# A transformer block planned offline: new cost constants for the planner that orders every engine

## Chip, core and metric

The kernel runs on one core of one Trainium2 chip. The metric is the device time of one execution in microseconds. Three runs of the kernel before took 1159.46, 1160.88 and 1164.24, median 1160.88.

## What is computed

One pre-norm transformer block over 2048 tokens of width 1024, batch 1, in bf16. Attention has 32 query heads of width 32 that share one key head and one value head. The feed-forward part has width 3584 and a sigmoid gate.

```python
def _A_ref(x, wq, wk, wv, wo):                      # H = 32, Dh = 32
    q = (x @ wq).reshape(B, S, H, Dh) ...           # x is layer-normed
    k = x @ wk ; v = x @ wv                         # one head for all
    p = softmax(einsum("bhqd,bkd->bhqk", q, k) * Dh ** -0.5)
    return einsum("bhqk,bkd->bhqd", p, v) ... @ wo

def _B_ref(x, w_gate, w_up, w_down):
    return (sigmoid(x @ w_gate) * (x @ w_up)) @ w_down

h  = x + _A_ref(_layernorm(x), wq, wk, wv, wo)
h2 = h + _B_ref(_layernorm(h), w_gate, w_up, w_down)
```

## The kernel before

Tokens are cut into 16 tiles of 128. Attention goes through *visits*. A visit is one step over 256 keys for two groups of four heads and one token tile: eight score matmuls into PSUM (`S_ps`, written by `emit_S`) and two exponentials of 128x1024 on ScalarE (line 571, `exps`) that write the tile `Pr`. There are 512 visits, 32 per token tile, and 1024 exponentials. `S_ps` has three pairs of banks, and a visit uses two of them, so the scores of a visit wait for the first exponential of the visit before (`deps.append(exps[2 * v - 2])` in `s_ready`).

Everything else that TensorE does is fitted between the scores of successive visits:

- PV blocks (`mk_PV`, `emit_PV`): 32 matmuls of `Pr` with the values `Vb`, two blocks for each eight visits. The second of the two also has eight matmuls with `ones` that sum the running totals `Ts`, from which the softmax's denominators come. `Ts` is added up on VectorE (line 601). When a block is done, VectorE empties its bank: line 633 for the first block; lines 637 and 639 (`Oc`, `Rc`) for the second.
- "Z" matmuls (named `zone` in the first part of the program): key, value and query projections of the whole sequence.
- OP (`mk_OP`): 16 matmuls per token tile with `wo_sb`.
- GU (`mk_GU`): gate and up projection, 14 groups of eight 512-wide matmuls per token tile. Their weights come in pieces of 256 KB over SP's queue (line 775) into the slots `ring` and, at the end, `Pr`. The gate half is followed by a tanh on ScalarE (line 817), the up half by a multiplication on VectorE (line 821), and a transposing DMA (line 825) turns the product for the next step.
- D (`mk_D`): down projection, two groups of 28 matmuls per token tile, with `hact` and `zone`.

PV, Z, OP, GU and D share two PSUM banks (`F_ps`): a group runs into one bank while the other is emptied. TensorE executes in order, so what waits there holds up all that stands behind it, the next scores included.

The order of all engines is written when the program is built, by the class `Plan`. Each operation has a cost: `occ`, how long it holds its engine, and `lat`, when its result is there. The planner advances a clock per engine and picks what its costs say is ready. The main loop emits the scores of a visit when ScalarE's planned backlog is under 750 ns, and otherwise takes a matmul of the group at hand. Where nothing is ready in the plan it emits filler matmuls (`ident` with `kT`) or lets its clock go on. Loads of weight pieces are put in line by `pump`, which looks at the planned state of the DMA queue; each load then waits for the matmul that frees its slot and for one exponential (`beat`). At run time only the order and the semaphores remain; the planned times are gone.

The functions that give the costs are `t_act` (ScalarE), `t_dve` (VectorE) and `t_mm` (TensorE); scores and PV blocks have costs of their own in `emit_S` and `emit_PV`, among them a sum added to `pl.free["pe"]` for the switch between kinds of matmul; a DMA's cost stands in `Plan.step`, from the bytes that its issuer names.

Of the kernel before, what the change touches and what calls it, by code (L numbers as in the profile page):

```python
# [13 lines left out]
P = 128  # L14
DH = 32
LN_EPS_BF16 = 1.0013580322265625e-05
SEM = 75.0
# [19 lines left out]
class Plan:  # L37
# [39 lines left out]
    def step(self, limit):  # L77
        best = None
        for e in self.ENG:
            h = self.heap[e]  # L80
            if h:
                s = max(self.free[e], min(o.ready for o in h))
                if best is None or s < best[0]:
                    best = (s, e)
        if best is None or (limit is not None and best[0] > limit):
            return False
        s, e = best
        h = self.heap[e]
        o = min((o for o in h if o.ready <= s + 1e-9), key=lambda o: (o.prio, o.seq))
        h.remove(o)  # L90
        self.free[e] = s + o.occ
        if o.nbytes:
            go = max(s + 1300.0, self.dma_free[e])
            self.dma_free[e] = go + o.nbytes / 280.0
            o.end = self.dma_free[e] + 700.0
        else:
            o.end = s + o.lat
        o.pos = len(self.lists[e])
        self.lists[e].append(o)
        for u in o.users:  # L100
# [14 lines left out]


def t_act(n):
    return dict(occ=n / 1.2 + 93.0, lat=n / 1.2 + 186.0 + SEM)


def t_dve(n, rate=0.96, fix=158.0):
# [1 line left out]


def t_mm(n):
    return dict(occ=max(25.0, n / 2.4 + 2.0), lat=max(25.0, n / 2.4 + 2.0) + 170.0 + SEM)


def bass_sequential_preLN__grouped_kv_mqa__glu_gated_glu__prompt_kernel(
# [12 lines left out]
    Bsz, S, D = A_x.shape  # L142
# [6 lines left out]
    FW = 512  # L149
# [11 lines left out]
    NST = 3  # L161
# [7 lines left out]
    with ExitStack() as es:  # L169
# [18 lines left out]
        hn = SB("hn", [D])  # L188
        hnT = SB("hnT", [2, DT, P])
# [212 lines left out]

        def dma_xT(t):
            xT_ev[t] = dma(lambda: SP.dma_start_transpose(
                out=xnT4[t // 4][:, :, (t % 4) * P:(t % 4 + 1) * P], in_=x_sb[:, t, :]), f"xT{t}", P * D * 2,
                [xnorm[t]], prio=0, occ=1330.0)
            xT_pe[t] = xT_ev[t]
            queue_after_xT(t)
# [138 lines left out]
        def emit_S(v):  # L547
            G, kq = visits[v]
            qb, g = G // ND, 2 * (G % ND)
            deps = s_ready(v)  # L550
            pl.free["pe"] += 95.0
            last = None
            for kk in range(KB):
                for j in range(4):
                    kt = kq * KB + kk
                    bank = 2 * ((2 * v + j // 2) % NB) + j % 2
                    last = pl.op("pe", mm(S_ps[:, bank, kk * 256:(kk + 1) * 256], kT4[DH * j:DH * (j + 1), kt * P:(kt + 1) * P],
                                          QTb[DH * j:DH * (j + 1), qb % 2, g:g + 2, :], True, True,
                                          tile_position=(DH * j, 0)),
                                 deps if (kk == 0 and j == 0) else [], occ=27.3, lat=27.3 + 190.0 + SEM)  # L560
            pl.free["pe"] += 95.0
            for i in range(2):
                u = 2 * v + i
                slot = u % NPS
                own = slot_owner.get(slot)
                free = [pv_done[own], slot_add[slot]] if own is not None else []
                slot_owner[slot] = (G, kq // VPH)
                slot_add[slot] = None
                slot_of[(G, kq, i)] = slot
                pb = 2 * (u % NB)  # L570
                exps[u] = pl.op("act", lambda slot=slot, pb=pb: ACT.activation(  # L571
                    out=Pr[:, slot, :].rearrange("p (a b) -> p a b", a=2), in_=S_ps[:, pb:pb + 2, :],
                    func=ACTF.Exp, scale=SCALE), [last] + free, prio=3, **t_act(1024))
# [92 lines left out]
        def emit_PV(t):  # L666

            banks = [b for b in range(2) if (cur is None or b != cur_b) and known(bank_rel[b], t)]
            if not banks or not queues["PV"]:
                return False  # L670
            gr = queues["PV"][0]
            if not gr.gate() or not known(gr.first(), t):
                return False
            queues["PV"].popleft()
            b = min(banks, key=lambda b: max([0.0] + [o.end for o in bank_rel[b]]))
            deps = gr.first() + list(bank_rel[b])
            for fn in gr.atoms(b):
                o = pl.op("pe", fn, deps, occ=27.3, lat=27.3 + 220.0 + SEM)
                o.tag = "PV"
                deps = []  # L680
            pl.free["pe"] += 95.0
            bank_rel[b] = gr.after(b, o)
            return True

# [40 lines left out]
        def flush_hT():  # L725
            while late_hT and (late_hT[0] < 2 or (late_hT[0] - 2) in gu_last):
                t = late_hT.pop(0)
                hT_ev[t] = dma(lambda t=t: SP.dma_start_transpose(
                    out=hnT[:, t % 2, :, :], in_=hn[:, :]), f"hT{t % 2}", P * D * 2,
                    [hnorm[t], gu_last.get(t - 2)], prio=0, occ=1330.0)  # L730
                for i in range(NI):
                    queues["GU"].append(mk_GU(t, i))
# [55 lines left out]
        def mk_GU(t, i):  # L788
            p, w = ITEMS[t * NI + i]
            n = t * NFP + i // 2  # L790
            its = [(p, w, d) for d in range(NPI)]

            def ready():
                if not all(it in held and piece_ld[it] for it in its):
                    return None
                return [piece_ld[it][0] for it in its]

            def atoms(b):
                sl = [held[it] for it in its]
# [12 lines left out]
            def after(b, last):  # L812
                if i == NI - 1:
                    gu_last[t] = last
                    flush_hT()
                if w == 0:
                    tanh_of[n] = pl.op("act", lambda: ACT.activation(  # L817
                        out=tnh[:, n % 2, :], in_=F_ps[:, b, :], func=ACTF.Tanh, scale=0.5),
                        [last, tn_user.get(n % 2)], prio=1, **t_act(FW))
                    return [tanh_of[n]]  # L820
                e = pl.op("dve", lambda: DVE.scalar_tensor_tensor(  # L821
                    out=hst[:, n % NST, :], in0=tnh[:, n % 2, :], scalar=1.0, in1=F_ps[:, b, :],
                    op0=ALU.add, op1=ALU.mult), [last, tanh_of[n], st_ev.get(n - NST)], prio=0, **t_dve(FW))
                tn_user[n % 2] = e
                st_ev[n] = dma(lambda: SP.dma_start_transpose(
                    out=hactT[:, t % 2, 4 * p:4 * p + 4, :], in_=hst[:, n % NST, :]), f"ha{n % NST}", P * FW * 2,
                    [e] + ([d_last[t - 2]] if t > 1 else q_store[-NQS:]), prio=0, occ=800.0)
                for f in range(4 * p, 4 * p + 4):
                    hact_ev[(t, f)] = st_ev[n]
                if i == NI - 1:  # L830
                    for dc in range(2):
                        queues["D"].append(mk_D(t, dc))
                return [e]
            gr = Group("GU", atoms, lambda: [hT_ev[t]] + ready()[:2], after)
            gr.gate = lambda: ready() is not None and (q_left[0] == 0 if t == 0 else (t < 2 or d_done[t - 2] == 2))
            return gr
# [217 lines left out]
```

## Time and profile before

| what | value |
|---|---|
| median of three runs | 1160.88 us |
| the profiled execution | 1161.15 us |
| its span, first to last instruction | 1159.4 us |
| granted TensorE clock, mean | 0.995 |
| TensorE / ScalarE / VectorE busy | 93% / 90% / 76% |
| DMA queue of SP, share of 16 engines | 73.4% |
| moved by DMA | 226.79 MB |

The page splits the span by engine, follows back the chain of work that ended last, and groups instructions by line; the groups give the mean length of one instruction, from its start to its end, although neighbours on one engine overlap. The timeline puts instructions of one kind that follow each other into one row: start, length from the first start to the last end, engine, line, names, count, and in brackets the idle time ahead of the row with what ended it. A few per cent of the matmul records are missing, so that a row can have one matmul less than the program. A row of stretches has start and end, length, then for each engine the busy time and the count of instructions, then the granted clock, the DMA share and GB/s; asked for the tile `S_ps`, it counts the score matmuls (TensorE and its weight loads) and the exponentials (ScalarE) alone.

### The profile page before, as it was taken

How to read it: one execution, taken by the hardware profiler on the slowest of the kernel's cores; microseconds unless marked ns; L12 is line 12 of the kernel's file. 1: busy time of each engine (PE TensorE's matmuls, PEld its weight loads, DVE VectorE, ACT ScalarE, POOL GpSimd, SP SyncE). 2: the span in 40 equal slices, each digit the busy share in tenths (PEclk: the TensorE clock that was granted, in tenths of full speed). 3: DMA queues.
4: the chain of work that ended last, by engine and by line, in shares of the span. 5: the costliest groups of instructions: out<-in, count | busy, mean ns of one | idle time of the engine just before them, and what ended most of it. 6: DMA issues, size and time to landing. Idle time of an engine off the chain costs nothing.

```text
span 1159.4 us, 30239 instructions
## 1 busy us (share of the span) xinstructions
PE 1078.7 (93%) x12193; PEld 482.9 (42%) x12374; DVE 877.8 (76%) x1688; ACT 1045.5 (90%) x1167; POOL 55.7 (5%) x84
## 2 busy tenths in 40 slices
PE   9899898889899999999899999999999999999998
PEld 5643344334343443434343443434344433444443
DVE  8889977777787878878697878878797868877511
ACT  6899998989999999999999999999999999999310
POOL 4100000000000000000000000000000000000000
PEclk9999999999999999999999999999999999999999
DMA  8675387876849587785959597785959587776993
GB/s 246 131 240 177 97 260 215 225 217 160 231 118 259 151 222 198 178 234 145 228 123 260 148 226 194 178 234 145 230 121 263 143 227 193 178 223 166 253 269 118
DMA packets 304283, 226.79 MB, mean 196 GB/s; under 512 B 117520, under 2 KB 295440, under 8 KB 304144
## 3 DMA queue, kind: packets, MB, share of 16 engines
q1 hardware_dynamic: 302064, 224.73, 73.4%
q8 instruction: 97, 1.59, 0.6%
q10 hardware_dynamic: 2080, 0.13, 0.1%
q14 instruction: 42, 0.34, 0.1%
HBM read 195.43 MB, written 7.86 MB: 175 GB/s over the span
## 4 chain that ended last, share of the span: by engine, by line
PE 61%; ACT 19%; DMA 7%; DVE 7%; issue 5%; POOL 0%; SPq 0%; POOLq 0%; DVEq 0%; ACTq 0%
PE F_ps L379 50%; ACT Pr L571 18%; PE S_ps L379 11%; DMA ring<-in_B_w_up_dram 6%; DVE Ts L601 3%; ACT tnh L817 1%; DMA ring<-in_B_w_gate_dram 1%; DVE Oc L637 1%; DVE Rc L639 1%; DVE hst L821 0%; DVE Rc L642 0%; DVE hact L267 0%; PE F_ps L384 0%; DVE Ri L640 0%; POOL dsb L339 0%
## 5 line engine op out<-in xcount | busy, mean ns | idle before, releaser
L571 ACT ACTIVATE Pr<-S_ps 128x1024 bf16<-128x1024 f32 x1024 | 979.0, 1029 | 30.9 <-PE S_ps L379 24.2
L601 DVE TENSOR_TENSOR Ts<-Ts,Pr 128x1024 bf16<-128x1024 bf16 x768 | 506.1, 679 | 64.2 <-ACT Pr L571 62.3
L379 PE MATMUL F_ps<-ring,hnT 128*128 128x512 bf16 x1654 | 411.0, 380 | 36.5 <-issue 13.5
L379 PEld LDWEIGHTS F_ps<-ring,hnT 128*128 128x128 bf16 x1760 | 152.0, 98 | 245.1 <-issue 71.9
L379 PE MATMUL S_ps<-QTb,kT 32*128 32x256 bf16 x4096 | 203.8, 273 | 18.7 <-issue 10.4
L379 PE MATMUL F_ps<-zone,hact 128*128 128x512 bf16 x842 | 207.3, 380 | 5.1 <-issue 4.5
L601 DVE TENSOR_TENSOR Ts<-Pr 128x1024 bf16<-128x1024 bf16 x128 | 87.2, 682 | 111.1 <-ACT Pr L571 111.0
L379 PEld LDWEIGHTS S_ps<-QTb,kT 32*128 32x128 bf16 x4096 | 60.7, 92 | 197.6 <-ACT Pr L571 130.4
L379 PE MATMUL F_ps<-Pr,Vb 128*32 128x256 bf16 x4096 | 137.0, 276 | 1.3 <-DVE hact L267 0.9
L379 PEld LDWEIGHTS F_ps<-zone,hact 128*128 128x128 bf16 x896 | 77.9, 98 | 105.8 <-issue 30.9
L817 ACT ACTIVATE tnh<-F_ps 128x512 f32<-128x512 f32 x112 | 68.1, 608 | 50.5 <-PE F_ps L379 50.5
L379 PEld LDWEIGHTS F_ps<-Pr,Vb 128*32 128x32 bf16 x4096 | 98.2, 97 | 33.1 <-issue 17.2
L821 DVE SCALAR_TENSOR_TENSOR hst<-tnh,F_ps 128x512 bf16<-128x512 f32 x112 | 75.4, 673 | 23.3 <-PE F_ps L379 23.1
L379 PE MATMUL F_ps<-zone 128*128 128x256 bf16 (+2 forms) x499 | 74.5, 291 | 5.1 <-DVE hact L267 2.1
L379 PE MATMUL F_ps<-wo_sb,OT 128*128 128x512 bf16 x252 | 62.7, 381 | 8.8 <-DVE Rc L639 7.6
L334 POOL TENSOR_SCALAR zb<-mvb 128x1 bf16<-128x1 bf16 (+1 forms) x25 | 11.7, 469 | 1040.5 <-DVE mvb L330 1040.4
L379 PEld LDWEIGHTS F_ps<-zone 128*128 128x128 bf16 x512 | 37.5, 98 | 33.7 <-issue 8.9
L851 DVE SCALAR_TENSOR_TENSOR h_sb<-F_ps,h_sb 128x512 bf16<-128x512 f32 x32 | 21.6, 677 | 33.9 <-PE F_ps L379 33.9
L379 PEld LDWEIGHTS F_ps<-wo_sb,OT 128*128 128x128 bf16 x256 | 21.4, 98 | 38.2 <-DVE Rc L639 10.7
L637 DVE TENSOR_TENSOR Oc<-F_ps,Oc 128x256 f32<-128x256 f32 x64 | 26.8, 419 | 12.5 <-PE F_ps L379 12.4
L633 DVE COPY Oc<-F_ps 128x256 f32<-128x256 f32 x64 | 27.0, 421 | 10.1 <-PE F_ps L379 9.8
L639 DVE STREAM_TRANSPOSE Rc<-F_ps 128x256 f32<-128x256 f32 x64 | 28.1, 439 | 0.0
(48 smaller groups left out, 359.3 us busy)
## 6 DMA issues: line engine op xcount, KB each, us to landing
ring<-in_B_w_gate_dram SPq DMA_DIRECT2D x320, 256.0 KB, 3.9
ring<-in_B_w_up_dram SPq DMA_DIRECT2D x319, 256.0 KB, 3.6
zone<-in_B_w_down_dram SPq DMA_DIRECT2D x28, 256.0 KB, 3.8
h_sb<-in_A_x_dram SPq DMA_DIRECT2D x16, 256.0 KB, 5.0
out_dram<-h_sb SPq DMA_DIRECT2D x32, 128.0 KB, 3.0
QTb<-q_scratch SPq DMA_DIRECT2D x14, 256.0 KB, 3.9
q_scratch<-hact SPq DMA_DIRECT2D x24, 128.0 KB, 2.5
ring<-in_A_x_dram SPq DMA_DIRECT2D x5, 512.0 KB, 7.0
```

Source lines behind the costliest of these rows:

```text
L334: f = pl.op("pool", lambda: POOL.tensor_scalar(out=zb[:, ph, sl].unsqueeze(2), in0=mvb[:, ph, sl, 1:2], scalar1=LN_EPS_BF16, scalar2=None, ...
L379: return lambda: PE.matmul(o, lhsT=l, rhs=r, start=start, stop=stop, **kw)
L571: exps[u] = pl.op("act", lambda slot=slot, pb=pb: ACT.activation(out=Pr[:, slot, :].rearrange("p (a b) -> p a b", a=2), in_=S_ps[:, pb:pb ...
L601: o = pl.op("dve", lambda T=T, a=a, b=b: DVE.tensor_tensor(out=T, in0=a, in1=b, op=ALU.add), deps, prio=4, **t_dve(1024, 1.92))
L633: oc_ev[G] = pl.op("dve", lambda: DVE.tensor_copy(out=Oc[:, :], in_=O), [last, o_ev.get(G - 1)], prio=0, **t_dve(256))
L637: a = pl.op("dve", lambda: DVE.tensor_tensor(out=Oc[:, :], in0=O, in1=Oc[:, :], op=ALU.add), [last, oc_ev[G]], prio=0, **t_dve(256))
L639: c = pl.op("dve", lambda: DVE.transpose(out=Rc[:, :], in_=R), [last, o_ev.get(G - 1)], prio=0, **t_dve(256))
L817: tanh_of[n] = pl.op("act", lambda: ACT.activation(out=tnh[:, n % 2, :], in_=F_ps[:, b, :], func=ACTF.Tanh, scale=0.5), [last, tn_user.get ...
L821: e = pl.op("dve", lambda: DVE.scalar_tensor_tensor(out=hst[:, n % NST, :], in0=tnh[:, n % 2, :], scalar=1.0, in1=F_ps[:, b, :], op0=ALU.a ...
L851: e = pl.op("dve", lambda: DVE.scalar_tensor_tensor(out=h_sb[:, t % 4, sl], in0=F_ps[:, b, :], scalar=0.5, in1=h_sb[:, t % 4, sl], op0=ALU ...
```

## The change

Only constants of the planner are altered. Nothing is added to or removed from the arithmetic.

| constant | before | after |
|---|---|---|
| exponential of 1024, `occ` | 946 ns | 913 ns |
| tanh of 512, `occ` | 520 ns | 487 ns |
| 512-wide matmul, `occ` | 215.3 ns | 216.0 ns |
| one score matmul, `occ` and the rest of `lat` | 27.3, 265 ns | 27.4, 225 ns |
| one PV matmul, `occ` | 27.3 ns | 27.4 ns |
| behind a visit's scores | 95 ns | 111 ns |
| behind a PV block | 95 ns | 109 ns |
| DMA: start, landing | 1300, 700 ns | 1400, 900 ns |
| bytes named for a transposing DMA | 2 per element | 2.5 per element |
| queue in which a DMA is counted | its issuer's | SP's for all |

```diff
         if o.nbytes:
-            go = max(s + 1300.0, self.dma_free[e])
-            self.dma_free[e] = go + o.nbytes / 280.0
-            o.end = self.dma_free[e] + 700.0
+            go = max(s + 1400.0, self.dma_free["sp"])
+            self.dma_free["sp"] = go + o.nbytes / 280.0
+            o.end = self.dma_free["sp"] + 900.0
...
 def t_act(n):
-    return dict(occ=n / 1.2 + 93.0, lat=n / 1.2 + 186.0 + SEM)
+    return dict(occ=n / 1.2 + 60.0, lat=n / 1.2 + 170.0 + SEM)
...
 def t_mm(n):
-    return dict(occ=max(25.0, n / 2.4 + 2.0), lat=max(25.0, n / 2.4 + 2.0) + 170.0 + SEM)
+    return dict(occ=max(25.0, n / 2.4 + 2.7), lat=max(25.0, n / 2.4 + 2.7) + 170.0 + SEM)
...
-                out=hnT[:, t % 2, :, :], in_=hn[:, :]), f"hT{t % 2}", P * D * 2,
+                out=hnT[:, t % 2, :, :], in_=hn[:, :]), f"hT{t % 2}", P * D * 5 // 2,
...
-                                 deps if (kk == 0 and j == 0) else [], occ=27.3, lat=27.3 + 190.0 + SEM)
-            pl.free["pe"] += 95.0
+                                 deps if (kk == 0 and j == 0) else [], occ=27.4, lat=27.4 + 150.0 + SEM)
+            pl.free["pe"] += 111.0
...
-                o = pl.op("pe", fn, deps, occ=27.3, lat=27.3 + 220.0 + SEM)
+                o = pl.op("pe", fn, deps, occ=27.4, lat=27.4 + 220.0 + SEM)
                 o.tag = "PV"
                 deps = []
-            pl.free["pe"] += 95.0
+            pl.free["pe"] += 109.0
```

The two other transposing DMAs (`dma_xT`, and the one of `hst`) get the same 5 // 2.

What it does to the order is shown on TensorE, at three places of one of the tiles from the middle of the program, which repeat from tile to tile. `S_ps<-QTb,kT` are the scores that begin a visit, `ring,hnT` is GU, `zone,hact` is D, `wo_sb,OT` is OP, `Pr,Vb` and `Ts,ones` are a PV block.

The first place, TensorE at the end of a tile's GU work ahead of D, before the change:

```order
L379 MATMUL S_ps<-QTb,kT 128x256 x8
L379 MATMUL F_ps<-ring,hnT 128x512 x10
L379 MATMUL S_ps<-QTb,kT 128x256 x8
L379 MATMUL F_ps<-ring,hnT 128x512 x5
L379 MATMUL S_ps<-QTb,kT 128x256 x8
L379 MATMUL F_ps<-Pr,Vb 32x256 x32
L379 MATMUL F_ps<-Ts,ones 32x256 x8
L379 MATMUL F_ps<-ring,hnT 128x512
L379 MATMUL S_ps<-QTb,kT 128x256 x8
L379 MATMUL F_ps<-ring,hnT 128x512 x3
```

The same place on TensorE after it:

```order
L379 MATMUL S_ps<-QTb,kT 128x256 x8
L379 MATMUL F_ps<-ring,hnT 128x512 x9
L379 MATMUL S_ps<-QTb,kT 128x256 x8
L379 MATMUL F_ps<-ring,hnT 128x512 x3
L379 MATMUL F_ps<-zone,hact 128x512 x3
L379 MATMUL S_ps<-QTb,kT 128x256 x8
L379 MATMUL F_ps<-zone,hact 128x512 x7
L379 MATMUL S_ps<-QTb,kT 128x256 x8
L379 MATMUL F_ps<-Pr,Vb 32x256 x32
L379 MATMUL F_ps<-Ts,ones 32x256 x8
L379 MATMUL F_ps<-zone,hact 128x512
```

The visits of five and of three GU matmuls are gone; GU work of the tile at hand ends two visits earlier, and the PV block stands beside D.

The second place, TensorE where OP begins, before the change:

```order
L379 MATMUL F_ps<-Pr,Vb 32x256 x32
L379 MATMUL F_ps<-Ts,ones 32x256 x8
L379 MATMUL F_ps<-zone,hact 128x512
L379 MATMUL S_ps<-QTb,kT 128x256 x8
L379 MATMUL F_ps<-wo_sb,OT 128x512 x3
L379 MATMUL S_ps<-QTb,kT 128x256 x8
L379 MATMUL F_ps<-wo_sb,OT 128x512 x7
```

The same place on TensorE after it:

```order
L379 MATMUL F_ps<-Pr,Vb 32x256 x32
L379 MATMUL F_ps<-zone,hact 128x512 x2
L379 MATMUL S_ps<-QTb,kT 128x256 x8
L379 MATMUL F_ps<-zone,hact 128x512 x7
L379 MATMUL S_ps<-QTb,kT 128x256 x8
L379 MATMUL F_ps<-zone,hact 128x512 x2
L379 MATMUL F_ps<-wo_sb,OT 128x512 x4
```

OP stood right behind a block with `ones`, one matmul and one set of scores away; it now follows a block without them, with eleven matmuls and two sets of scores between.

The third place, TensorE in the GU work of the next tile, around the block with `ones`, before the change:

```order
L379 MATMUL S_ps<-QTb,kT 128x256 x8
L379 MATMUL F_ps<-Pr,Vb 32x256 x32
L379 MATMUL F_ps<-Ts,ones 32x256 x8
L379 MATMUL F_ps<-ring,hnT 128x512 x2
L379 MATMUL S_ps<-QTb,kT 128x256 x8
L379 MATMUL F_ps<-ring,hnT 128x512 x6
```

The same place on TensorE after it:

```order
L379 MATMUL S_ps<-QTb,kT 128x256 x8
L379 MATMUL F_ps<-ring,hnT 128x512 x3
L379 MATMUL F_ps<-Pr,Vb 32x256 x32
L379 MATMUL F_ps<-Ts,ones 32x256 x8
L379 MATMUL S_ps<-QTb,kT 128x256 x8
L379 MATMUL F_ps<-ring,hnT 128x512 x5
```

The block now stands behind three GU matmuls of its visit; of the five that follow the scores, two end a group and three begin the next one, in the bank that the block has used.

In the whole program, fillers go from 87 to 57 and weight loads from 655 to 649. Behind the scores of the last visit stand 158 GU matmuls where 148 stood; the numbers of D, OP and PV matmuls there are the same.

More of the change, by code (lines that the diff above doesn't have):

```diff
@@ L404, in dma_xT @@
             xT_ev[t] = dma(lambda: SP.dma_start_transpose(
-                out=xnT4[t // 4][:, :, (t % 4) * P:(t % 4 + 1) * P], in_=x_sb[:, t, :]), f"xT{t}", P * D * 2,
+                out=xnT4[t // 4][:, :, (t % 4) * P:(t % 4 + 1) * P], in_=x_sb[:, t, :]), f"xT{t}", P * D * 5 // 2,
                 [xnorm[t]], prio=0, occ=1330.0)
@@ L825, in after @@
                 st_ev[n] = dma(lambda: SP.dma_start_transpose(
-                    out=hactT[:, t % 2, 4 * p:4 * p + 4, :], in_=hst[:, n % NST, :]), f"ha{n % NST}", P * FW * 2,
+                    out=hactT[:, t % 2, 4 * p:4 * p + 4, :], in_=hst[:, n % NST, :]), f"ha{n % NST}", P * FW * 5 // 2,
                     [e] + ([d_last[t - 2]] if t > 1 else q_store[-NQS:]), prio=0, occ=800.0)
```

## Prediction, made before the changed kernel was run

> **What bounds the kernel now.** I read the page first, then ScalarE and TensorE in order of time inside one token tile, then the stretches between fixed points of the program.
>
> ```profile
> span 1159.4 us, 30239 instructions
> PE 1078.7 (93%) x12193; PEld 482.9 (42%) x12374; DVE 877.8 (76%) x1688; ACT 1045.5 (90%) x1167; POOL 55.7 (5%) x84
> PE 61%; ACT 19%; DMA 7%; DVE 7%; issue 5%; POOL 0%; SPq 0%; POOLq 0%; DVEq 0%; ACTq 0%
> L571 ACT ACTIVATE Pr<-S_ps 128x1024 bf16<-128x1024 f32 x1024 | 979.0, 1029 | 30.9 <-PE S_ps L379 24.2
> ```
>
> TensorE is busy 93%, ScalarE 90%, and the chain that ends last changes between them, so two engines are near their limit. The 1029 ns of one exponential is not its price: in order of time, successive ones overlap.
>
> ```profile
> 424.20 3.77 ACT L571 ACTIVATE Pr<-S_ps 128x1024 bf16<-128x1024 f32 x4
> ...
> 480.51 0.59 ACT L817 ACTIVATE tnh<-F_ps 128x512 f32<-128x512 f32 x1
> 480.99 5.93 ACT L571 ACTIVATE Pr<-S_ps 128x1024 bf16<-128x1024 f32 x6
> ```
>
> Four in 3.77 us make a distance of (3.77 - 1.03) / 3 = 0.913 us; six in 5.93 us make (5.93 - 1.03) / 5 = 0.98, and the additional 0.07 is waiting. So "busy" hides ScalarE's waits, and its real need is 0.913 per exponential and 480.99 - 480.51 = 0.48 per tanh. Where the time goes is seen on TensorE.
>
> ```profile
> 51.32 1.70 PE L379 MATMUL F_ps<-zone 128*128 128x256 bf16 x14
> ...
> 756.80 0.40 PE L379 MATMUL S_ps<-QTb,kT 32*128 32x256 bf16 x8
> 757.13 0.60 PE L379 MATMUL F_ps<-ring,hnT 128*128 128x512 bf16 x2
> 758.04 1.09 PE L379 MATMUL F_ps<-ring,hnT 128*128 128x512 bf16 x3 [0.30 <-DMA ring<-in_B_w_up_dram]
> 759.06 0.40 PE L379 MATMUL S_ps<-QTb,kT 32*128 32x256 bf16 x8
> 759.38 1.06 PE L379 MATMUL F_ps<-Pr,Vb 128*32 128x256 bf16 x32
> 760.27 0.39 PE L379 MATMUL F_ps<-Ts,ones 128*32 128x256 bf16 x8
> 760.91 0.40 PE L379 MATMUL S_ps<-QTb,kT 32*128 32x256 bf16 x8 [0.25 <-issue]
> 762.04 0.81 PE L379 MATMUL F_ps<-ring,hnT 128*128 128x512 bf16 x3 [0.74 <-DVE Rc L639]
> 762.78 0.40 PE L379 MATMUL S_ps<-QTb,kT 32*128 32x256 bf16 x8
> ...
> 765.16 0.40 PE L379 MATMUL S_ps<-QTb,kT 32*128 32x256 bf16 x8
> 765.49 1.69 PE L379 MATMUL F_ps<-zone,hact 128*128 128x512 bf16 x7
> 767.11 0.40 PE L379 MATMUL S_ps<-QTb,kT 32*128 32x256 bf16 x8
> 767.44 1.06 PE L379 MATMUL F_ps<-Pr,Vb 128*32 128x256 bf16 x32
> ...
> 768.97 0.40 PE L379 MATMUL S_ps<-QTb,kT 32*128 32x256 bf16 x8
> ...
> 775.80 0.82 PE L379 MATMUL F_ps<-wo_sb,OT 128*128 128x512 bf16 x3 [0.69 <-DVE Rc L639]
> ...
> 1093.02 3.62 PE L379 MATMUL F_ps<-wo_sb,OT 128*128 128x512 bf16 x16
> ```
>
> Every S_ps row begins a visit. Prices follow from rows without waits: a 512-wide matmul (3.62 - 0.38) / 15 = 0.216 us, 0.38 being its own length; a 256-wide one (1.70 - 0.28) / 13 = 0.11. A visit with seven matmuls lasts 767.11 - 765.16 = 1.95, so its scores and both switches cost 1.95 - 7 x 0.216 = 0.44. A PV block costs 768.97 - 767.11 - 0.44 - 2 x 0.216 = 0.99 (the order has two matmuls behind it). With the eight ones matmuls it costs 760.91 - 759.06 - 0.44 - 0.22 = 1.19. Three visits of this tile are far longer than their work: the one at 756.80 waits for a weight piece, and those before 762.04 and 775.80 wait until VectorE has emptied the PSUM bank of a block just finished (1.38 us from the end of the ones matmuls, 760.66, to 762.04).
>
> ```profile
> 30.73:96.06 65.33, 12.71 (x256) 3.82 (x257) 59.56 (x64) 0.97 0.68 190
> 96.06:160.02 63.96, 12.71 (x257) 3.80 (x258) 60.58 (x65) 1.00 0.55 162
> 160.02:229.28 69.26, 12.71 (x256) 3.79 (x256) 61.20 (x65) 1.00 0.79 221
> 229.28:297.80 68.52, 12.96 (x257) 3.81 (x258) 61.14 (x65) 0.98 0.77 200
> 297.80:364.04 66.24, 12.92 (x256) 3.80 (x256) 61.16 (x65) 0.97 0.69 184
> 364.04:1015.12 651.08, 127.08 (x2560) 37.90 (x2561) 613.24 (x641) 1.00 0.75 193
> 1015.12:1079.81 64.69, 12.32 (x248) 3.67 (x249) 60.19 (x63) 1.00 0.78 200
> 1079.81:1159.40 79.59, 0.40 (x8) 0.12 (x8) 1.95 (x3) 1.00 0.80 212
> ```
>
> These are stretches of 32 visits (256 score matmuls), the sixth ten tiles at once, the seventh 31 visits, the last all that follows the last scores. A steady tile takes 65.1 us.
>
> **What the change does.** It alters only the planner's constants, so it acts through the order. Arithmetic is the same, but TensorE issues 30 filler matmuls fewer, SP six weight loads fewer (655 to 649), and one key and one value copy go from ScalarE to VectorE in the first stage.
>
> *Steady tiles.* In both orders a tile holds 32 visits, 184 matmuls (112 GU, 56 D, 16 OP) and eight PV blocks, four with ones: 32 x 0.44 + 184 x 0.216 + 4 x 0.99 + 4 x 1.19 = 62.5 us of TensorE. ScalarE needs 64 x 0.913 + 7 x 0.48 = 61.8. The 65.1 therefore hold 2.6 of TensorE waits. The old order has two visits of three matmuls (1.09 us) against ScalarE's 1.83, and one of five (1.52) that waits for a piece. The new one has none under 1.52: most are 1.74 to 1.95, and those with a tanh 2.17 to 2.38 against 2.31. Adding for each visit the larger of the two needs gives 64.8 before and 64.1 after, an upper end without other waits; the lower is 62.5. I take a value near the lower end. Thirteen new visits are shorter than ScalarE's need, twelve by 0.18 at most and one by 0.31, and they alternate with longer ones. Scores may run ahead, because three pairs of score banks let a visit start when the first exponential of the last one ends, one exponential (0.91) less the scores' 0.44 early. A shortfall within that is made up by the next visit.
>
> To this I add bank waits. OP now starts two sets of scores and eleven matmuls behind a PV block without ones, so the wait of 0.69 goes. But one GU group starts two matmuls and a visit (0.87) behind a ones block, another 1.30 behind, against the 1.38 needed: 0.5 and 0.1. Weight pieces: I followed in both programs which matmul and which exponential each load waits for, and which matmul first uses it. The shortest lead, in visits, between release and first use goes from 1.5 to 3.0 per steady tile. The landing takes
>
> ```profile
> ring<-in_B_w_gate_dram SPq DMA_DIRECT2D x320, 256.0 KB, 3.9
> ```
>
> 3.9 us, two visits, so three cover it and 1.5 do not. If that cover fails, the 0.7 that the visit at 756.80 loses now (759.06 - 756.80 less 1.52) returns. A tile: 62.5 + 0.6 = 63.1, and ten give 631, minus 20.
>
> The Trainium skill weighs against this: "ScalarE: Activation LUTs", section "What ACT_TABLE_LOAD costs", gives an ACTIVATE with immediates 186 ns + 0.833 ns per element and an overlap of about 93 ns between neighbours, which makes 946 ns here, the figure that the old planner used. The row of four above has 0.913, shorter than that. With 946 and 520 for a tanh the page would make a tile 64.2 by ScalarE alone, an estimate.
>
> *Other stages,* each as TensorE's need, ScalarE's need, sum of maxima, by the same prices:
>
> | stretch | before, taken | after | I take |
> |---|---|---|---|
> | 1st | 57.3, 58.4, 63.1; 65.3 | 59.9, 58.4, 65.5 | 65.3 |
> | 2nd | 60.6, 59.9, 63.9; 64.0 | 57.8, 59.9, 63.0 | 61.5 |
> | 3rd | 62.3, 62.3, 66.1; 69.3 | 61.2, 62.3, 64.8 | 65.5 |
> | 4th | 63.8, 61.8, 65.2; 68.5 | 62.3, 61.8, 64.5 | 63.8 |
> | 5th | 61.3, 61.8, 64.5; 66.2 | 62.5, 61.8, 64.1 | 63.1 |
> | 31 visits | 63.7, 60.5, 64.1; 64.7 | 60.7, 60.0, 62.5 | 61.8 |
>
> The first waits for x arriving, which no order hastens: unchanged (63 to 67). The second and the 31 visits are put between the bounds. The third and fourth run over the old bound by 3.2 and 3.3 through late pieces. With 19 pieces in place of 30 led by 2.5 visits or less, I leave the third 2.0 over the middle of its bounds; in the fourth, whose least lead rises from 1 to 2, 0.4. Such a wait is paid twice:
>
> ```profile
> 233.67 0.39 PE L379 MATMUL F_ps<-ring,hnT 128*128 128x512 bf16 x1 [2.10 <-DMA ring<-in_B_w_gate_dram]
> 233.99 0.54 PE L379 MATMUL S_ps<-QTb,kT 32*128 32x256 bf16 x8
> 234.47 1.90 PE L379 MATMUL F_ps<-Pr,Vb 128*32 128x256 bf16 x32
> ```
>
> After 2.10 us of waiting the PV block took 1.90 instead of 1.06. *The tail* has ten GU matmuls more than before (158 for 148): 79.6 + 10 x 0.216 = 81.8. VectorE's two copies lie in the first stage's range.
>
> Sum, with 30.7 to the first scores: 30.7 + 65.3 + 61.5 + 65.5 + 63.8 + 63.1 + 631.0 + 61.8 + 81.8 = 1124.5 us of span, 34.9 under 1159.4. The profiled execution took 1161.15, 1.75 more than its span, and lies 0.27 over the median of 1160.88. So the time is 1126.0.
>
> **Rivals.** (1) *No averaging:* every visit costs the larger need. Eleven tiles lose 1.0 each, the second stretch 1.5, the fourth and the 31 visits 0.7 each: 1140. For it: the old tile's 65.1 is near its own sum of maxima; against: there nearly all full visits are TensorE's, so nothing could average. (2) *ScalarE bounds:* if half of the 0.07 that the row of six has over the row of four is its own and no wait, an exponential needs 0.947, a tile 64 x 0.947 + 3.4 = 64.0, and the time is that of rival 1. For it: rows like that of six are the more frequent; against: the row of four could not stand beside it. The Trainium skill's figure above would lead here. (3) *The plan does not reach the chip:* late pieces come back at other visits with their 2.6 us per tile: 1160. Against: twice the lead. (4) *Slower, by late sums:* the ones matmuls need VectorE's running sums; if these come late, scores are queued behind them on TensorE and ScalarE starves.
>
> ```profile
> PEld F_ps L379 <- DVE Ts L601: 5.1, 24, 0.2
> ```
>
> In the ten tiles this was 0.2 at most, 24 times. The steady saving is 2.0 a tile, so from 0.5 per ones block, four a tile, it decides; at 1.0, 14 tiles of 4.0 turn 1126 into 1182.
>
> **Chances.** Forecast 0.74, (1) 0.13, (2) 0.04, (3) 0.04, (4) 0.05. Both sides of 0.5%, 5.8 us, which is about what a measurement here can tell: faster 0.74 + 0.13 + 0.04 = 0.91, same 0.04, slower 0.05. Low end: tiles at 62.5, the first stretches 2 each better, 1112. High end: rival (1) with the third stretch 3 worse, 1143. Cases 3 and 4 stay out.
>
> **What would show it.** Right: ten steady tiles of 62.5 to 63.5, no wait for weight pieces in them, no OP wait for Rc, one GU wait of about 0.5, a last stretch near 82. Wrong: a tile over 64, exponentials that follow at 0.94 without a wait between them, waits for pieces after 300 us, or a tail over 85 with waits for pieces.

## Result and profile after

The changed kernel takes 1125.45 us (median of four runs, 1123.86 to 1127.85) against 1162.05 for the kernel before in the same comparison: ratio 0.9688, 95% interval 0.9658 to 0.9717. The profiled execution took 1126.47 us, 1.77 more than its span.

The page of the kernel after, with span, busy shares, the chain that ended last and the exponentials' group:

```profile
span 1124.7 us, 30157 instructions
PE 1069.6 (95%) x12163; PEld 478.9 (43%) x12347; DVE 873.7 (78%) x1690; ACT 1022.9 (91%) x1165; POOL 49.1 (4%) x84
PE 82%; ACT 5%; DVE 5%; issue 5%; DMA 2%; POOL 0%; SPq 0%; DVEq 0%; ACTq 0%
L571 ACT ACTIVATE Pr<-S_ps 128x1024 bf16<-128x1024 f32 x1024 | 961.9, 1056 | 18.2 <-PE S_ps L379 15.3
```

The chain was 61% TensorE and changed hands; now it is 82%, with DMA down from 7% to 2% and ScalarE from 19% to 5%. The stretches of 32 visits, cut at the same visits as before (start and end in us, length; then, for score matmuls and exponentials alone, busy time and count of TensorE, of weight loads and of ScalarE; clock, DMA share, GB/s):

```profile
30.44:96.29 65.85, 12.71 (x256) 3.85 (x257) 58.57 (x64) 1.00 0.75 207
96.29:161.17 64.88, 12.71 (x256) 3.79 (x257) 60.45 (x65) 1.00 0.53 153
161.17:227.65 66.48, 12.93 (x257) 3.82 (x259) 60.81 (x64) 0.97 0.82 223
227.65:291.38 63.73, 12.70 (x257) 3.79 (x258) 59.78 (x65) 1.00 0.84 220
291.38:354.14 62.76, 12.71 (x256) 3.78 (x257) 60.14 (x65) 1.00 0.83 199
354.14:981.76 627.62, 127.04 (x2560) 37.87 (x2560) 601.47 (x641) 1.00 0.78 200
981.76:1043.63 61.87, 12.31 (x249) 3.68 (x250) 58.15 (x63) 1.00 0.68 185
1043.63:1124.70 81.07, 0.40 (x8) 0.11 (x8) 2.53 (x3) 1.00 0.74 196
```

The ten steady tiles give 651.08 - 627.62 = 23.5 of the 34.7 us of span, the third to fifth stretches 11.1, the 31 visits 2.8; the first two stretches lose 1.4 together, the tail 1.5. Each steady tile now repeats in 62.76 us.

A part of the third to fifth stretches is the clock of TensorE. In the after, the granted clock is half of full speed from 162.0 to 165.4 us, right behind a wait for a piece that ends at 160.85 (a row of all engines: TensorE, weight loads, VectorE, ScalarE, GpSimd, then clock, DMA share, GB/s):

```profile
162.00:165.40 3.40, 3.40 (x43) 1.77 (x45) 0.84 (x2) 2.77 (x4) 0.00 (x0) 0.50 0.85 247
```

The trace of the kernel before has the same 3.4 us at half clock twice in these stretches, from 234.1 and from 302.4, beside waits for pieces of 2.10 and 2.25 us. This is why the PV block in the prediction's row at 234.47 took 1.90 us in place of 1.06. As an estimate, 3.4 us at half clock cost 1.7 us of TensorE's work, and one such time fewer is 1.7 of the 11.1. Not every long wait is followed by one: late4, below, waits 2.03 us at 940.55 without it. In the ten tiles the clock is 1.00 in both kernels.

What TensorE waits for in those ten tiles, with sum, times and longest, before:

```profile
PE F_ps L379 <- DVE Rc L639: 11.3, 16, 0.7
PE F_ps L379 <- DMA ring<-in_B_w_up_dram: 5.3, 12, 1.1
PE S_ps L379 <- DMA ring<-in_B_w_gate_dram: 0.8, 3, 0.3
```

and after, the whole answer:

```profile
PE F_ps L379 <- issue: 12.4, 70, 0.3
PE S_ps L379 <- issue: 5.1, 20, 0.3
PE S_ps L379 <- ACT Pr L571: 2.5, 10, 0.3
```

The 17.4 us put down to emptied banks and weight pieces are gone. What remains is hardly waiting: a tile has 184 matmuls of 512 in the program and 173 in this trace, and all but one of its ten brackets, 0.16 to 0.26 long, stand where a record is missing. OP's 16 matmuls, for one, are rows of 4, 7 and 4 with a bracket of 0.16 ahead of the last. The places of the prediction's timeline, in the kernel after:

```profile
731.04 2.12 PE L379 MATMUL F_ps<-ring,hnT 128*128 128x512 bf16 x9
...
733.42 0.82 PE L379 MATMUL F_ps<-ring,hnT 128*128 128x512 bf16 x3
734.08 0.81 PE L379 MATMUL F_ps<-zone,hact 128*128 128x512 bf16 x3
...
744.93 1.03 PE L379 MATMUL F_ps<-wo_sb,OT 128*128 128x512 bf16 x4
...
785.34 0.39 PE L379 MATMUL F_ps<-Ts,ones 128*32 128x256 bf16 x8
785.66 0.40 PE L379 MATMUL S_ps<-QTb,kT 32*128 32x256 bf16 x8
786.00 0.39 PE L379 MATMUL F_ps<-ring,hnT 128*128 128x512 bf16 x1
786.67 0.81 PE L379 MATMUL F_ps<-ring,hnT 128*128 128x512 bf16 x3 [0.28 <-issue]
```

GU's end runs into D without a bracket, OP starts without a wait for `Rc`, and the only bank wait of size lies in the 0.28 ahead of the GU group at 786.67 (one of the two matmuls ahead of it is missing in the trace). The page names no releaser there; on VectorE, line 639, which empties the bank, ends at 786.57 (its row stands below).

### The profile page after: what moved, and what is told of

Its sections match the earlier page's. It is cut to its first block, busy times and chain, and to the rows that moved or that the text cites. A ratio compares the mean times of both kernels' runs of the same rounds, so it can differ in the third digit from the quotient of the medians.

```text
span 1124.7 us, 30157 instructions
## 1 busy us (share of the span) xinstructions
PE 1069.6 (95%) x12163; PEld 478.9 (43%) x12347; DVE 873.7 (78%) x1690; ACT 1022.9 (91%) x1165; POOL 49.1 (4%) x84
## 4 chain that ended last, share of the span: by engine, by line
PE 82%; ACT 5%; DVE 5%; issue 5%; DMA 2%; POOL 0%; SPq 0%; DVEq 0%; ACTq 0%
PE F_ps L379 69%; PE S_ps L379 14%; ACT Pr L571 5%; DVE Ts L601 2%; DMA ring<-in_B_w_gate_dram 1%; DMA ring<-in_B_w_up_dram 1%; DVE st L320 1%; DVE st L322 1%; ACT ring L363 0%; DVE ring L359 0%; DMA ring<-in_A_x_dram 0%; DVE hact L267 0%; ACT tnh L817 0%; DVE Rc L639 0%; POOL rstd L341 0%
## 5 line engine op out<-in xcount | busy, mean ns | idle before, releaser
L571 ACT ACTIVATE Pr<-S_ps 128x1024 bf16<-128x1024 f32 x1024 | 961.9, 1056 | 18.2 <-PE S_ps L379 15.3
L379 PE MATMUL S_ps<-QTb,kT 32*128 32x256 bf16 x4096 | 203.5, 273 | 14.5 <-ACT Pr L571 7.0
L817 ACT ACTIVATE tnh<-F_ps 128x512 f32<-128x512 f32 x112 | 71.1, 635 | 50.4 <-PE F_ps L379 50.4
L379 PE MATMUL F_ps<-wo_sb,OT 128*128 128x512 bf16 x240 | 59.8, 380 | 3.1 <-issue 2.1
L642 DVE STREAM_TRANSPOSE Rc<-Ri 128x256 f32<-128x256 f32 x64 | 27.9, 436 | 0.0
```

Of the source, the lines that this page charges most:

```text
L379: return lambda: PE.matmul(o, lhsT=l, rhs=r, start=start, stop=stop, **kw)
L642: d = pl.op("dve", lambda: DVE.transpose(out=Rc[:, :], in_=Ri[:, :].unsqueeze(2).to_broadcast([P, 2 * P // DH, DH])), [r], prio=2, **t_dve ...
L817: tanh_of[n] = pl.op("act", lambda: ACT.activation(out=tnh[:, n % 2, :], in_=F_ps[:, b, :], func=ACTF.Tanh, scale=0.5), [last, tn_user.get ...
```

## Experiments

All twelve further kernels, with the two of the case. "Ten tiles" is the stretch of ten steady tiles (320 visits), "rest" the span less that. Ratios are against the kernel before, measured beside each; its median was 1160.7 to 1162.4. The intervals of pe_only and nobeat_before reach 1, so these two cannot be told from the kernel before.

| kernel | median us | ratio, interval | ten tiles | rest |
|---|---|---|---|---|
| before | 1162.05 | 1 | 651.1 | 508.3 |
| after | 1125.45 | 0.9688 [0.9658, 0.9717] | 627.6 | 497.1 |
| act_only | 1146.22 | 0.9863 [0.9833, 0.9894] | 639.3 | 505.5 |
| pe_only | 1160.28 | 0.9992 [0.9978, 1.0005] | 655.7 | 504.4 |
| dma_only | 1166.06 | 1.0042 [1.0018, 1.0066] | 661.4 | 501.8 |
| no_act | 1146.67 | 0.9867 [0.9833, 0.9901] | 639.9 | 503.5 |
| no_pe | 1140.73 | 0.9806 [0.9776, 0.9835] | 633.1 | 506.2 |
| no_dma | 1155.07 | 0.9941 [0.9917, 0.9965] | 651.1 | 501.2 |
| nobeat_before | 1159.30 | 0.9984 [0.9966, 1.0001] | 650.7 | 506.6 |
| ql_later | 1152.81 | 0.9916 [0.9884, 0.9948] | 645.6 | 504.3 |
| nobeat_after | 1125.11 | 0.9700 [0.9663, 0.9737] | 627.6 | 495.7 |
| late2 | 1127.57 | 0.9710 [0.9695, 0.9725] | 627.9 | 498.0 |
| late4 | 1146.30 | 0.9861 [0.9835, 0.9887] | 643.6 | 503.1 |
| tuned | 1111.83 | 0.9560 [0.9527, 0.9594] | 624.6 | 485.2 |

My theory was the prediction's: what was saved is waits of TensorE, and an order is free of them when no visit is much too short and each weight piece is released early enough. Its rivals: one constant does it alone (the price of the exponential above all), the pacing wait of the loads does it, or the rows that stand beside a piece do.

**One group of constants at a time.** The three groups are the exponential's and tanh's costs (`act`), TensorE's costs (`pe`) and the transfers' (`dma`). act_only is the kernel before with

```diff
-    return dict(occ=n / 1.2 + 93.0, lat=n / 1.2 + 186.0 + SEM)
+    return dict(occ=n / 1.2 + 60.0, lat=n / 1.2 + 170.0 + SEM)
```

and no_act is the kernel after with that line undone; pe_only, dma_only, no_pe and no_dma do the same with the lines of `t_mm`, `emit_S` and `emit_PV`, and with `Plan.step` and the three transposes' bytes.

> The kernel before with the new cost of exponentials and tanh alone (occ 913 and 487). Its order, priced with the rows of the profile before: 62.5 us of TensorE per steady tile, leads of three visits, but one visit of 0.87 us (two GU matmuls behind a ones block) and one of 1.52: tile about 63.4, total about 1132. Rival (the price of the exponential is the whole change): 1125, within 3. Rival (it does nothing without the switch costs): above 1150.

> The changed kernel with the old cost of exponentials and tanh (946 and 520); switches and transfers stay new. Its order has two visits of 1.09 us per tile, 0.74 under ScalarE's need, and a least lead of two visits against a landing of 3.9 us: tile about 64.0, total about 1142. Rival (the exponential's price is the whole change): back to 1158 to 1162. Rival (it hardly matters): 1128 or less.

> The kernel before with TensorE's new costs alone. In its order a steady tile has one visit of 0.66, leads of 1.0 to 1.5 visits and a sum of the larger needs of 65.2. Theory (as for transfers alone): tile 64.5 to 66, time 1146 to 1156. Rival (the groups add up, and TensorE's costs were worth 15 when taken out of the after): 1146 at most.

> The kernel before with the new costs of transfers alone. In its order TensorE keeps the old short visits (three of 1.09 in a steady tile, sum of the larger needs 65.2) and gets fillers, while the least lead is 1.0. Theory (each of the three groups of costs helps only when the other two let it: without the exponential's new cost the tiles stay at their sum of the larger needs): tile 65 to 66, time 1150 to 1162. Rival (the groups add up, and transfers were worth 30 when taken out of the after): 1131.

> The kernel after with TensorE's old costs alone (switches 95, matmul 215.3, score and PV matmul 27.3, latency 190). In its order one visit of a steady tile has three matmuls (1.09), the least lead of a piece is 2 visits, and the tail holds some 1.4 more work. Theory (a short visit behind which a bank must be emptied costs about 0.7 in each tile): tile 63.4, time about 1134. Rival (a single short visit is made up by the next, as three pairs of score banks allow): tile 62.8, time about 1127.

> The kernel after with the old costs of transfers alone (start 1300, landing 700, 2 bytes per element, a queue each). In its order a steady tile has one visit of three matmuls again (1.52 with what stands beside them) and pieces that are led by 1.0 visit at least. Theory (the transfer costs decide how early pieces are asked for, and a lead of one visit does not cover a landing of two): a steady tile of 64.0 to 64.6 with a wait for a piece, time about 1141. Rival (transfers' costs matter only in the first stages; ScalarE's and TensorE's costs carry the steady tile): tile 62.8, time 1123 to 1130.

The steady tiles of no_act came out as expected, 64.0, with two bank waits of about 0.8 in short visits; act_only's are 63.9 (63.4 expected), one wait of 0.8 and smaller ones. Its total was 14 over what I had written: some 5 of it are the tiles, most of the rest is in its first four stretches, which took 65 to 68. no_act's was 5 over; its third stretch took 70.1. no_pe's tiles were 63.0, two of them 64.2 and 64.6 with a wait for a piece. That lies between the theory (63.4) and the rival (62.8): its visit of three matmuls is not made up, but costs 0.57 and not 0.7. Its total missed by 7: the third stretch took 70.6, and the tail 86.6 where the after has 81.1 and I had allowed 1.4 more. no_dma lost twice what I expected: tiles at 65.1. Its ten tiles, and what TensorE waited for in them:

```profile
353.81:1004.92 651.11, 127.04 (x2560) 37.86 (x2561) 603.67 (x641) 1.00 0.76 193
PE F_ps L379 <- DMA ring<-in_B_w_up_dram: 7.0, 11, 1.3
PE F_ps L379 <- DMA ring<-in_B_w_gate_dram: 6.7, 10, 1.4
PE F_ps L379 <- DVE Rc L639: 3.6, 10, 0.4
```

So with the old costs of transfers pieces come late 21 times, and the whole gain of the steady tiles is lost. Yet the same costs alone made the kernel slower: dma_only's tiles are 66.1, with three visits of three matmuls, fillers between, and ten waits for pieces (8.1 us from 365 to 960 us); pe_only's are 65.6, with eleven waits for gate pieces (13.4 us there). Both times lie above the ranges I had written, so the sign against the rival (that groups add up) is plain and my sizes were too hopeful. The groups do not add up: alone they are worth -14.5, -1.9 and +3.8 us against before, together -36.6. Taken singly out of the after they cost 21, 15 and 30. No group has a price of its own; each only helps to an order in which both conditions of the theory hold. Which constant inside a group does it was not tested.

**The same order, pieces released later.** This takes the order out of the question: every instruction of the kernel after keeps its place, and only the exponential that a weight load waits for is moved by 2 or 4.

```diff
-        paced = collections.deque()
+        paced = collections.deque(); beats = []
...
-                sink.append(dma(fn, key, nbytes, list(deps) + [beat], prio=4))
+                sink.append(dma(fn, key, nbytes, list(deps) + [beat], prio=4)); beats.append((sink[-1], clock[0]))
...
+        for o, u in beats:
+            if 256 <= u < 940: o.deps = [exps[u + 4] if d is exps.get(u) else d for d in o.deps]
```

> The order of the kernel after on every engine, nothing moved; only the pacing exponential that a weight load waits for is two exponentials (one visit) later, for exponentials 256 to 939. The least lead of a piece in a steady tile falls from 3.0 visits to 2.0. Theory (a landing takes two visits, so two are the edge): most tiles stay at 62.8, some lose 1 to 1.6 at one visit as with TensorE's old costs; time 1126 to 1131. Rival (lead has nothing to do with it; the after's tiles are free of piece waits because of what stands beside them on TensorE): 1125.

> As the one before, with the pacing exponential four exponentials (two visits) later: least lead 1.0 visit, two pieces at 1.0 and two at 1.5 in each steady tile. Theory (lead against landing): waits for pieces return, 1.5 to 2.5 us in a tile, tiles at 64.3 to 65.2 and the time 1142 to 1152, although no instruction has another place. Rival (lead has nothing to do with it): 1125.

late2's tiles are 62.76 as in the after, nine in 564.87 us with no matmul of GU waiting for a piece; its total cannot be told from the after's (the intervals overlap). late4's nine tiles, and the pieces waited for in them:

```profile
358.93:937.15 578.22, 114.35 (x2305) 34.10 (x2307) 542.78 (x577) 1.00 0.78 196
PE F_ps L379 <- DMA ring<-in_B_w_up_dram: 8.2, 14, 1.3
PE F_ps L379 <- DMA ring<-in_B_w_gate_dram: 1.4, 2, 1.0
```

The first place where it waits, the visit of nine GU matmuls that the after runs in one row of 2.12 (731.04 above):

```profile
359.26 2.10 PE L379 MATMUL F_ps<-ring,hnT 128*128 128x512 bf16 x8
362.62 0.39 PE L379 MATMUL F_ps<-ring,hnT 128*128 128x512 bf16 x1 [1.27 <-DMA ring<-in_B_w_up_dram]
```

A lead of two visits is enough here; one and one and a half, the two shortest in late4, are not: 1.5 us a tile, 13.4 in nine, and 1146.3 in place of 1125. Lead is shown to be a cause by itself, as large in a tile as taking out the exponential's costs (1.2). Not all of late4's loss is lead: of the 22.0 us of span that it has over the after, 16.0 lie in the ten tiles and 1.1 in the 31 visits, but 3.5 lie in the third stretch (69.9), whose loads the edit does not reach. That part is open.

**Which wait made the old tile long.** In nobeat_before and nobeat_after the loads no longer wait for an exponential at all, only for their slot (the last line below in place of late2's); the order stays.

```diff
+        for o, deps in beats: o.deps = [d for d in deps if d is not None]
```

> The order before, on every engine, with one thing taken away: weight loads no longer wait for an exponential as their pace, only for their slot. Theory (order plus leads): of the 2.6 us that a steady tile loses before, about 1.0 is a late weight piece and 1.5 are the two waits for a PSUM bank that VectorE empties. Without the pace the piece comes at least two visits ahead, so the tile goes from 65.1 to about 64.4 and the visit of five GU matmuls to about 1.83 us; the third to fifth stretch lose some 10 us of waits; total near 1143. The two bank waits of 0.7 stay. Rival (pieces explain it all): the tile falls to 63 and the time to about 1130. Rival (pieces are bound by transfer rate, not by when they are released): no change, 1160.

> The changed order with the same pace taken away. Theory: steady tiles have no piece waits left, so they stay at 62.8; the second to fourth stretch (64.9, 66.5, 63.7) still wait for pieces, 2.7 us at one visit, and lose perhaps 5 us; total near 1120. Rival (transfer rate): pieces released early collide with others, 1125 or more.

nobeat_before stayed at 65.07 a tile, a miss of 16 us: its time is the one of the rival that knows only the transfer rate. The pieces of the visit of five were still late, and SP's queue suggests another reason:

```profile
751.14 1.30 SPq L516 DMA_DIRECT2D QTb<-q_scratch  x1
752.48 1.17 SPq L775 DMA_DIRECT2D ring<-in_B_w_up_dram  x2
```

```profile
756.68 1.11 PE L379 MATMUL F_ps<-ring,hnT 128*128 128x512 bf16 x3 [0.40 <-DMA ring<-in_B_w_up_dram]
```

The two up pieces stand behind the load of the next queries (`QTb`, line 516), which waits for the tile's last scores; no earlier release of their own helps them. ql_later is nobeat_before with that load put behind the weight loads that follow it:

```diff
+        sp = pl.lists["sp"]; i = 0
+        while i < len(sp):
+            n = 0
+            if sp[i].key and sp[i].key.startswith("ql"):
+                while n < 2 and i + n + 1 < len(sp) and sp[i + n + 1].key and sp[i + n + 1].key.startswith("sl"): n += 1
+                sp.insert(i + n, sp.pop(i))
+            i += n + 1
```

> The kernel before, its weight loads without the wait for the pacing exponential, and on SP's queue each load of QTb moved behind the up to two weight loads that followed it. TensorE's order is that of before. Theory (the GU visit of five waits for an up piece because SP stands at the QTb load, which waits for the tile's last scores): that wait goes, the two waits for an emptied bank (0.8 each) stay; a steady tile falls from 65.05 to about 64.3, ten tiles give 7, and the time is about 1150. Rival (the weight queue itself is behind, so the piece comes late whatever stands ahead of it): tile 65.0 again, time 1158 to 1160.

Its SP queue, and TensorE at the visit of five and behind it:

```profile
745.49 2.33 SPq L775 DMA_DIRECT2D ring<-in_B_w_up_dram  x3
747.86 0.56 SPq L516 DMA_DIRECT2D QTb<-q_scratch  x1
```

```profile
750.66 1.25 PE L379 MATMUL F_ps<-ring,hnT 128*128 128x512 bf16 x5
...
753.07 0.39 PE L379 MATMUL F_ps<-Ts,ones 128*32 128x256 bf16 x8
753.71 0.40 PE L379 MATMUL S_ps<-QTb,kT 32*128 32x256 bf16 x8 [0.26 <-ACT Pr L571]
755.15 0.81 PE L379 MATMUL F_ps<-ring,hnT 128*128 128x512 bf16 x3 [1.04 <-DVE Rc L639]
```

The five matmuls run in one row, the tile falls to 64.45 in most cases (64.3 was expected), and the theory of the blocked queue holds. Whether moving the load would do without the earlier release was not tested. But the wait behind the ones block grew from 0.74 to 1.04. VectorE shows what the bank really waits for, in before, after and ql_later at the same PV block's end or its like:

```profile
760.56 0.69 DVE L601 TENSOR_TENSOR Ts<-Ts,Pr 128x1024 bf16<-128x1024 bf16 x1 [0.65 <-ACT Pr L571]
```

```profile
785.11 0.69 DVE L601 TENSOR_TENSOR Ts<-Ts,Pr 128x1024 bf16<-128x1024 bf16 x1 [0.72 <-ACT Pr L571]
...
786.13 0.44 DVE L639 STREAM_TRANSPOSE Rc<-F_ps 128x256 f32<-128x256 f32 x1
```

```profile
753.66 0.69 DVE L601 TENSOR_TENSOR Ts<-Ts,Pr 128x1024 bf16<-128x1024 bf16 x1 [0.22 <-ACT Pr L571]
```

Each is a running sum of 0.69 that ends only after the ones matmuls (these end at 760.66, 785.73 and 753.46), and the two operations that empty the bank, lines 637 and 639, follow it. From the ones' end to the next group it took 1.38, 0.94 and 1.69 us: the same work, met by the sum at another moment. This also tells the bank from ScalarE, whose need of 1.83 could hold a visit of three matmuls just as long: the visit lasts 1.87 in before (760.91 to 762.78), but 2.18 in ql_later (753.71 to 755.89) and 1.66 in no_pe, so it goes by the bank.

In the after, removing the pacing changed the steady tiles by nothing and the total by nothing measurable, where I had expected 5 us less. The second stretch fell from 64.9 to 63.6, but the third rose to 67.0, with five waits for pieces, 4.0 us together; the median landing of a gate piece rose from 3.8 to 4.7 us. So the rival, that pieces released early collide, describes these stretches of this order better than my theory. That the bytes are no bound for every order is shown by the next version.

**A version with the rest of the constants set nearer to the trace.**

```diff
-            go = max(s + 1400.0, self.dma_free["sp"])
-            self.dma_free["sp"] = go + o.nbytes / 280.0
-            o.end = self.dma_free["sp"] + 900.0
+            go = max(s + 1494.0, self.dma_free["sp"])
+            self.dma_free["sp"] = go + o.nbytes / 275.0
+            o.end = self.dma_free["sp"] + 849.0
...
-def t_dve(n, rate=0.96, fix=158.0):
+def t_dve(n, rate=0.96, fix=145.0):
...
-    PACE = 205.0
+    PACE = 256.0
...
-            while paced and t >= next_piece[0] and pl.dma_free["sp"] < t + 2500.0:
+            while paced and t >= next_piece[0] and pl.dma_free["sp"] < t + 4485.0:
...
-                if can_s and run - t < 750.0:
+                if can_s and run - t < 820.0:
```

Beside these, `lat` behind a visit's scores is 27.4 + 197 (+ 150 before), its switch 104 (111), PV's 113 (109).

> The kernel after with its remaining constants set nearer to what its trace shows: a transfer 1494 before it moves, 849 for landing, 275 bytes per ns; weight loads paced at 256 and asked for up to 4485 ahead; 197 behind the scores, switches of 104 and 113, a VectorE operation's fixed part 145, scores let in at a backlog of 820. In its order no steady visit is under 1.53, every piece is led by 4 visits or more, and by 20 in the second stretch. Theory (what is left over TensorE's need are late pieces in the first three stretches, some 7 us, and 0.3 of bank wait in each tile): stretches one to four lose their piece waits, the tile is 62.5, the tail 76 to 77, and the time 1112 to 1118. Rival (the early stretches wait for the queue's bytes and not for the order): the waits move and stay, tile 62.6, time 1122 to 1126.

It takes 1111.83 us, better than both kernels and just under the range I had written. Its second and third stretches and the ten tiles, and all that TensorE waits for in these:

```profile
95.58:155.94 60.36, 12.71 (x256) 3.78 (x257) 59.24 (x65) 1.00 0.52 152
155.94:219.55 63.61, 12.71 (x256) 3.79 (x256) 60.13 (x65) 1.00 1.04 272
...
344.97:969.54 624.57, 127.07 (x2562) 37.88 (x2563) 602.68 (x641) 1.00 0.78 202
PE F_ps L379 <- issue: 11.1, 70, 0.2
PE S_ps L379 <- ACT Pr L571: 5.1, 20, 0.3
PE S_ps L379 <- issue: 2.5, 10, 0.3
```

At 62.46 a tile is what TensorE's instructions need, worked out as 62.5 in the prediction. Nothing of waits is left in it: the 100 brackets of the ten tiles stand where the trace lacks a record (174 of 184 in each tile). ScalarE's need (61.3, below) stands close under it. From 30 to 291 us no piece is waited for, as the theory said. The tail came out at 79.7, not at 76 to 77. Against the after, the second to fourth stretches give 8.1, the eleven steady tiles 3.4, the 31 visits and the tail 2.7. Several constants moved at once, so no part of this belongs to one of them.

## Why the prediction was right, point by point

1126.0 was forecast, 1125.45 measured, and the cause is the one given: waits of TensorE that the new order does not have. That the sum fits to 0.2 us (1124.5 of span forecast, 1124.7 measured) is luck, as errors of some 5 us cancel in it.

- **The steady tile.** Forecast 63.1, measured 62.76. TensorE's need of 62.5 holds (tuned shows it bare), and the sum of the larger needs, 64.1, is not paid: a visit up to 0.3 shorter than ScalarE's need is made up by the next. Rival 1, no averaging, falls. What a bank costs in a visit of two or three matmuls is not made up: about 0.8 each in no_act and act_only, 0.57 in no_pe.
- **The bank waits.** This is the mis-sized term of the tile: 0.6 forecast, 0.3 measured. Where I had put 0.5, the visit lasts 1.75 (785.66 to 787.41) and its scores and five matmuls are priced at 1.52, so 0.23. Where I had put 0.1, the visit lasts its price (754.01 to 755.75 for six matmuls), so nothing; another 0.1 shows in a visit with a PV block between two matmuls (791.52), and no run shows why. I took 1.38 us from the ones' end as the bank's price; it holds the remainder of whatever sum VectorE has in hand and ranged from 0.94 to 1.69. Ten tiles came out 3.4 us under the forecast.
- **Weight pieces.** In the ten tiles none is waited for; after 300 us there are only three such waits, 2.0 us together, all behind 981 us, though I had named any such wait a sign of being wrong. "Three visits cover it and 1.5 do not" is borne out by late2 (2.0 covers) and late4 (1.0 and 1.5 do not). For the old order my reading was incomplete: a lead of 1.5 was not the whole cause, since without the pacing the piece stayed late, and ql_later shows that SP's order held it.
- **The second stretch** is the step that failed: 61.5 forecast, 64.88 measured. I put it midway between bounds that hold no wait for pieces, and priced no late piece in it. One visit, the last of the stretch, waits for an up piece that has a lead of one visit:

```profile
160.85 0.39 PE L379 MATMUL F_ps<-ring,hnT 128*128 128x512 bf16 x1 [2.47 <-DMA ring<-in_B_w_up_dram]
```

This is 2.5 of the 3.4 us; nobeat_after, where the same wait is 1.15, takes 63.56. The other 0.9 stays open. The third came out 1.0 over, although 2.0 were left in it for late pieces: the half clock behind this wait falls into it. The first came out 0.6 over, with no wait for a piece; why stays open. These 4.9 us too low were met by the tiles' 3.7 too high, and by 1.0 in the tail (81.07 for 81.8) and the start (30.44 for 30.7).
- **Rival 2, ScalarE at 0.947.** A row of exponentials in tuned with no bracket ahead of it, and the tanh behind it:

```profile
709.68 6.55 ACT L571 ACTIVATE Pr<-S_ps 128x1024 bf16<-128x1024 f32 x7
716.02 0.70 ACT L817 ACTIVATE tnh<-F_ps 128x512 f32<-128x512 f32 x1
716.50 4.81 ACT L571 ACTIVATE Pr<-S_ps 128x1024 bf16<-128x1024 f32 x5
```

(716.02 - 709.68) / 7 = 0.906 us, and 0.48 for the tanh; the seven distances, start to start, are 0.904 or 0.905 us but for one of 0.919. So the 0.07 of the old row of six was waiting, and ScalarE needs 64 x 0.906 + 7 x 0.48 = 61.3 a tile. The 946 ns that the prediction worked out from the Trainium skill ("ScalarE: Activation LUTs", section "What ACT_TABLE_LOAD costs") do not hold for these exponentials out of PSUM. The Trainium skill's "Perfetto Trace Analysis", section "Optimizing Scalar/DVE Operations", gives about 51 ns of overhead for ScalarE on PSUM; with the 0.833 ns per element of the former that makes, as an estimate, 904 ns and 478 ns. The trace agrees: 0.904 us and 0.48 us.
- **Rivals 3 and 4.** The plan reached the chip: the late pieces did not come back at other visits of the ten tiles. No wait for `Ts` shows on TensorE in the ten tiles.
- **No group alone.** The prediction priced the order and not the constants; the six runs on groups show that this was needed, since -14.5, -1.9 and +3.8 do not make -36.6.

What is argued and not shown: why exactly two pieces of no_pe's tiles, whose lead is also 2.0 visits, came late in two of ten tiles and those of late2 in none. The two orders differ in the transfers that stand beside them; no run separates that.

## What to carry to other kernels

Price the order that a planner writes, not the constants that are changed in it: add up the engine's need from rows without waits, then look for work that begins too soon behind a block whose bank must first be emptied, and for transfers released less than a landing ahead of their first use, in the irregular first stages as well as in the steady part. Where a piece is late, look at what stands ahead of it in its queue before its own release is moved. When one engine's bare need equals the measured tile, as in the steady tiles of the last version here, order has nothing left to give there, and only less work on that engine will. And before a bracket of the timeline is called a wait, compare the row's count with the program's: here most of the short ones are missing records.

## What the runs showed of the hardware

The steady tiles of the after and of tuned repeat to 0.01 us, ten times in a row, while tiles with late pieces vary: 63.4 to 64.7 in the nine of late4, with the same instructions in the same places. Behind some long waits the clock granted to TensorE was half for 3.4 us: from 162.0 us in the after, from 234.1 and 302.4 in the kernel before. nobeat_after and tuned, where TensorE waits 1.4 us or more nowhere behind 35 us, show no such time up to the end of their spans. One waiting load in SP's queue held back the two loads behind it; moving it (ql_later, 1152.81 against 1159.30 for nobeat_before, intervals of the ratio not overlapping) was worth 0.5 us a tile. And how long a PSUM bank takes to come free was set here by what VectorE had just begun: 0.94 to 1.69 us for the same two operations.
